# Transposing q of the first head pair of a batch by DMA instead of on TensorE, in a fused attention and feed-forward kernel

## The chip, the cores and the metric

The kernel runs on 1 core of one Trainium2 chip. The metric is the device time of one execution in microseconds (us), taken as the median of several runs. PE is TensorE, DVE is VectorE, ACT is ScalarE, POOL is GpSimd, and SP is the engine whose queue issues nearly all DMAs of this kernel.

## The reference

A thresholded attention over 8 batches and 8 heads of 576 rows and 64 columns feeds a two-layer block on 4608 rows of 512 columns. Cut to what matters:

```python
scores = (q @ k.transpose(0, 1, 3, 2)) / sqrt(64)        # per batch and head, 576 x 576
thresh = scores.max(-1, keepdims=True) - tau              # tau = 0.02
scores = where(scores >= thresh, scores, -1e9)
attn   = softmax(scores)
x      = (attn @ v), heads side by side                   # 4608 x 512
h      = x @ w_in                                         # 4608 x 2048
out    = (h - tanh(h)) @ w_out                            # 4608 x 512
```

## The kernel before

**Pairs, tiles and steps.** Two heads make a pair; there are 32 pairs p, four to a batch, so that pairs with `p % 4 == 0` are the first of a batch. A pair has nine tiles of 128 query rows: four of each head, and one that holds the last 64 rows of both (the shared tile). Tile i belongs to pair i // 9. A hand-written loop runs over steps s, and each step issues a piece of work for several tiles at once: `scores(s + 8)`, the kink of a tile three steps later, the exponential and the attention product of tiles further behind, and a share of the feed-forward work (`todo`). The order in which the loop issues is the order of every engine's queue; nothing is rescheduled afterwards.

**Preparing q and k.** `load` brings q, k and v of a pair from HBM through SP's queue. `split` (POOL, L189 to L193) scales the fp32 tile and writes it as two fp16 halves, high and low, into `qhl` or `khl`, so that 64 columns become 128. `turn` then transposes the nine 128 x 128 blocks. For k it does so on PE (L240, into the PSUM tile `ps_k`), DVE copies the result to `kT` (L263), and POOL makes a second copy with the two halves of the partitions exchanged, `kS` (L269, two instructions). For q there are two ways: like k through `ps_q` and a DVE copy to `qT`, or one DMA transpose straight from `qhl` to `qT` on SP's queue (L252). `q_by_dma(p)` chooses. The DMA writes the columns of the shared tile in another order, and `scores` reads them with a step of two (`qrem`).

**Scores and what follows.** A tile's scores are `kT` products followed by `kS` products into one PSUM tile `psS` (L331, L322 for the shared tile). DVE moves them to SBUF with the row maximum (L341) and derives the threshold `nb` (L353); ACT forms `z` (L368). From pair 6 on, two tiles' `z` are transposed by one DMA on SP's queue into `zT` (L375), and ACT takes the exponential into `pT` (L404), which PE multiplies with v (L425, L432, L443). The feed-forward block runs beside this: PE `psH` (L498), ACT `th` (L511), DVE `g` (L517), PE `psY` (L524). In each batch after the first it starts anew four steps after its first pair's step 0, so those four steps have no feed-forward work.

**When it is issued.** The table `PREP` and the lines behind it put `split` and `turn` into `plan`, at a distance d of steps ahead of step 9p - 8. For a pair p of 5 or more, `turn` of k stands at d = 6 for odd and d = 3 for even pairs. `turn` of q stands at d = 2, or at d = 7 if it goes by DMA, and both splits then stand two steps earlier:

```python
if d in (7, 8) and q_by_dma(p):
    d = d + 2
...
d = 7 if q_by_dma(p) else 3 - (p == 1 or p >= 5)
```

An engine's queue runs in order, so an instruction that waits holds up those behind it. Buffers: `hl`, `qk` (qT, kT, kS) and `ps_big` (psS, ps_q, ps_k) have two each.

Of the kernel before, what the change touches and what calls it, by code (L numbers as in the profile page):

```python
# [18 lines left out]
def kernel(  # L19
# [26 lines left out]
    HPAIR = H // 2  # L46
# [196 lines left out]

    def q_by_dma(p):

        return p >= 2 * HPAIR and p % 4 != 0

    def turn(p, t):
        hl = hls.pop((p, t))
        if t == "q" and q_by_dma(p):  # L250
            m = mats[p, t] = qk_pool.tile([P, W], FP16, name=f"{t}T", tag=t)
            nc.sync.dma_start_transpose(  # L252
                out=m.rearrange("p (c r) -> p c r", c=TPP),
                in_=hl.rearrange("p c a d -> p (c a d)"),
            )
            return
        ps = ps_big.tile([P, W], FP16, name=f"ps_{t}", tag="big")
        for c in range(TPP):
            turn_chunk(
                ps[:, c * P : (c + 1) * P], c, hl[:, c, :, :].rearrange("p a d -> p (a d)")  # L260
            )
        m = qk_pool.tile([P, W], FP16, name=f"{t}T", tag=t)
        nc.vector.tensor_copy(out=m, in_=ps)  # L263
        mats[p, t] = m
        if t == "k":
            sw = qk_pool.tile([P, W], FP16, name="kS", tag="ks")
            for lo, hi in ((0, D), (D, 0)):
                o, i = sw[lo : lo + D, :], m[hi : hi + D, :]
                nc.gpsimd.tensor_copy(out=o, in_=i)  # L269
            mats[p, "ks"] = sw  # L270
# [37 lines left out]
    def scores(i):  # L308
# [6 lines left out]
        if hh is None:  # L315
            qrem = REM
            if q_by_dma(p):
                qrem = (slice(512, 640, 2), slice(513, 640, 2))
            for n, kk in enumerate((kT, kS)):
                for dst, srcs in ((main, MAIN), (rem, REM)):  # L320
                    for hh in range(2):
                        nc.tensor.matmul(  # L322
                            out=ps[64 * hh : 64 * hh + 64, dst],
                            lhsT=qT[:, qrem[hh]], rhs=kk[:, srcs[hh]],
                            start=(n == 0), stop=(n == 1),
                        )
        else:
            lhs = qT[:, (5 * hh + t) * P : (5 * hh + t + 1) * P]
            for n, kk in enumerate((kT, kS)):
                for dst, src in ((main, MAIN[hh]), (rem, REM[hh])):  # L330
                    nc.tensor.matmul(  # L331
                        out=ps[:, dst], lhsT=lhs, rhs=kk[:, src],
                        start=(n == 0), stop=(n == 1),
                    )
# [324 lines left out]
    for p in range(1, NPAIR):  # L659
        first = TPP * p - AHEAD  # L660
        for d, f in PREP[3 if p == 1 else 0 :]:
            d -= p == 1 and d in (3, 5)
            if d in (7, 8) and q_by_dma(p):
                d = d + 2
            if p in (2, 4):
                d = {8: 9, 7: 8, 5: 6}.get(d, d)
            elif d == 5 and p >= 5:
                d = 6 if p % 2 else 3
            plan.setdefault(first - d, []).append(lambda p=p, f=f: f(p))
        d = 7 if q_by_dma(p) else 3 - (p == 1 or p >= 5)  # L670
        d = 4 if p in (2, 4) else d
        plan.setdefault(first - d, []).append(lambda p=p: turn(p, "q"))
# [30 lines left out]
    for s in range(-AHEAD, NTILE + LAG + 3):  # L703
        p, j = divmod(max(s, 0), TPP)
# [107 lines left out]
```

## Time and profile before

| | |
|---|---|
| median of 3 runs | 533.78 us (533.04, 533.78, 533.81) |
| the profiled execution's own time | 533.81 us, span 532.0 us |
| mean granted TensorE clock | 0.996 |
| busy share of the span | PE 96%, ACT 82%, DVE 79%, POOL 55% |
| DMA transposes `zT<-z` | 117, median 3.5 us from issue to landing |
| DMA transposes `qT<-qhl` | 18, median 3.3 us from issue to landing |
| q transposes on PE (`ps_q`, nine blocks each) | 126 matmuls, 14 pairs |

How to read it: the busy share of PE is an average over the whole span. Rows of the timeline give the start, the length, the engine, the line, the operation and the tile, and in brackets the idle time just before it with what ended it. A row that merges several instructions ends with their count. A matmul's length in such a row holds its latency; from the start of one group to the start of the next is what it takes of PE.

### The profile page before, as it was taken

To read this page: it belongs to the slowest core of one execution; us is meant where nothing else is said; L and a number is where in the kernel's file an instruction comes from. 1 tells how busy PE (TensorE), PEld (TensorE's weight loads), DVE (VectorE), ACT (ScalarE), POOL (GpSimd) and SP (SyncE) were. 2 spreads that over 40 slices of the span, in tenths; PEclk is the share of its full clock that TensorE was granted. 3 is DMA by queue.
4 is the path that set the end of the run, shared out by engine and by line. 5 is a ranking of instruction groups with operands and counts; after the bars stand their busy time and mean duration, and the time that the engine had idled before them with its cause. 6 is when DMAs were issued, how large, how long until landed. Compare 5 with 4: busy or idle time off the path is not lost.

```text
span 532.0 us, 12716 instructions
## 1 busy us (share of the span) xinstructions
PE 509.2 (96%) x4606; PEld 287.6 (54%) x4606; DVE 421.0 (79%) x1179; ACT 435.8 (82%) x617; POOL 290.1 (55%) x390
## 2 busy tenths in 40 slices
PE   8999899988999999999999999999999999999996
PEld 4666566544555555555555555555555555444444
DVE  5899879996888988898889988898889887554440
ACT  5999899988898989898898989898989899543330
POOL 8999989683746657475727574666657530000000
PEclk9999999998999999999999999999999999999999
DMA  7843659979897999789898899999979996400113
GB/s 212 252 133 114 217 186 184 167 160 197 170 209 140 190 184 217 173 179 202 186 197 186 191 188 199 171 185 199 214 160 185 195 149 110 105 33 28 39 41 80
DMA packets 208607, 86.79 MB, mean 163 GB/s; under 512 B 176160, under 2 KB 200992, under 8 KB 208544
## 3 DMA queue, kind: packets, MB, share of 16 engines
q1 hardware_dynamic: 207952, 85.56, 76.0%
q8 instruction: 36, 0.59, 0.5%
q10 hardware_dynamic: 592, 0.43, 0.3%
q14 instruction: 27, 0.22, 0.1%
HBM read 36.70 MB, written 9.44 MB: 87 GB/s over the span
## 4 chain that ended last, share of the span: by engine, by line
PE 35%; issue 20%; POOL 19%; ACT 9%; DMA 8%; DVE 6%; SPq 2%; POOLq 0%; ACTq 0%; DVEq 0%
PE psY L524 12%; PE psH L498 9%; PE psS L331 6%; POOL kS L269 5%; DMA vraw<-in_v_dram 4%; ACT z L368 3%; ACT pT L396 3%; PE psHt L498 3%; DMA kraw<-in_k_dram 3%; POOL khl L193 3%; POOL vb L221 2%; POOL qhl L193 2%; ACT th L511 1%; POOL qhl L192 1%; PE psO L432 1%
## 5 line engine op out<-in xcount | busy, mean ns | idle before, releaser
L341 DVE TENSOR_SCALAR_CACHE_REDUCE sc<-psS 128x576 f32<-128x576 f32 x288 | 214.2, 753 | 39.8 <-PE psS L331 25.9
L368 ACT ACTIVATE z<-sc,nb 128x576 bf16<-128x576 f32 x288 | 216.4, 772 | 22.2 <-DVE nb L353 20.3
L524 PE MATMUL psY<-w_out_sb,g 128*128 128x512 bf16 (+1 forms) x592 | 145.9, 373 | 0.8 <-DVE yo L537 0.8
L404 ACT ACTIVATE pT<-zT 128x1152 f16<-128x1152 bf16 x117 | 135.2, 1156 | 13.4 <-DMA zT<-z 13.2
L269 POOL COPY kS<-kT 64x1152 f16<-64x1152 f16 x62 | 70.9, 1144 | 125.9 <-DVE nb L353 124.4
L498 PE MATMUL psH<-xT,w_in_sb 128*128 128x512 bf16 x480 | 124.1, 381 | 2.6 <-DVE g L517 2.5
L331 PEld LDWEIGHTS <-qT 128*128 128x128 f16 x1024 | 74.8, 98 | 62.3 <-issue 8.4
L331 PE MATMUL psS<-kT,qT 128*128 128x512 f16 (+1 forms) x512 | 104.6, 286 | 3.2 <-DVE sc L341 1.2
L517 DVE SCALAR_TENSOR_TENSOR g<-th,psH 128x512 bf16<-128x512 f32 x128 | 87.6, 684 | 20.9 <-ACT th L511 20.4
L331 PE MATMUL psS<-kS,qT 128*128 128x512 f16 x496 | 101.6, 286 | 1.7 <-POOL kS L269 1.6
L511 ACT ACTIVATE th<-psH 128x512 f32<-128x512 f32 x128 | 74.8, 585 | 22.4 <-PE psH L498 21.8
L524 PEld LDWEIGHTS <-g 128*128 128x128 bf16 x592 | 51.0, 98 | 56.9 <-issue 2.4
L498 PEld LDWEIGHTS <-w_in_sb 128*128 128x128 bf16 x576 | 49.4, 98 | 57.9 <-issue 6.0
L432 PE MATMUL psO<-vb,pT 128*128 128x65 bf16 x1024 | 53.5, 194 | 0.0
L432 PEld LDWEIGHTS <-pT 128*128 128x128 f16 x1024 | 44.4, 98 | 9.7
L193 POOL TENSOR_TENSOR qhl<-qraw,qhl 128x576 f16<-128x576 f32 x31 | 39.7, 1281 | 2.6
L193 POOL TENSOR_TENSOR khl<-kraw,khl 128x576 f16<-128x576 f32 x31 | 39.7, 1281 | 2.6
L396 ACT ACTIVATE pT<-psZ 128x512 f16<-128x512 bf16 (+1 forms) x54 | 35.2, 655 | 3.9 <-PE psZ L387 3.5
L537 DVE COPY yo<-psY 128x512 f32<-128x512 f32 (+1 forms) x31 | 21.2, 682 | 14.1 <-PE psY L524 12.4
L425 PE MATMUL psO<-vb,pT 128*128 128x130 bf16 x128 | 28.3, 221 | 3.3 <-ACT pT L404 2.7
L458 DVE TENSOR_TENSOR osb<-psO,rc 128x256 bf16<-128x256 f32 x64 | 27.2, 424 | 2.2
L263 DVE COPY kT<-ps_k 128x1152 f16<-128x1152 f16 x31 | 23.3, 753 | 4.1 <-PE ps_k L240 4.1
(79 smaller groups left out, 508.8 us busy)
## 6 DMA issues: line engine op xcount, KB each, us to landing
vraw<-in_v_dram SPq DMA_DIRECT2D x32, 256.0 KB, 4.0
out_dram<-yo SPq DMA_DIRECT2D x32, 256.0 KB, 2.8
kraw<-in_k_dram SPq DMA_DIRECT2D x31, 256.0 KB, 3.2
qraw<-in_q_dram SPq DMA_DIRECT2D x31, 256.0 KB, 3.4
wt<-in_moe_w_in_dram SPq DMA_DIRECT2D x8, 512.0 KB, 4.6
wt<-in_moe_w_out_dram SPq DMA_DIRECT2D x8, 512.0 KB, 3.9
zT<-z SPq DMA_TRANSPOSE x117, 3.5
qraw<-in_q_dram SPq DMA_DIRECT2D x32, 32.0 KB, 3.3
```

The costliest lines, as they stand in the source:

```text
L193: nc.gpsimd.tensor_tensor(out=hl[:, :, 1, :], in0=x, in1=hl[:, :, 0, :], op=ALU.subtract)
L269: nc.gpsimd.tensor_copy(out=o, in_=i)
L331: nc.tensor.matmul(out=ps[:, dst], lhsT=lhs, rhs=kk[:, src], start=(n == 0), stop=(n == 1),)
L341: nc.vector.tensor_scalar(out=sc, in0=ps[:, lo : lo + S], scalar1=SC, scalar2=None, op0=ALU.mult, op1=ALU.max, accum_out=mx[:, c : c + 1],)
L368: nc.scalar.activation(out=z, in_=sc, func=ACT.Prelu, bias=nb, scale=1.0, alpha=STEEP)
L396: nc.scalar.activation(out=pt[:, off * P : (off + n) * P], in_=ps[:, 0 : n * P], func=ACT.Exp)
L404: nc.scalar.activation(out=pt[:, 0 : n * P], in_=zts.pop(i)[:, 0:n, :], func=ACT.Exp)
L432: nc.tensor.matmul(out=po[:, t - 1 + ab, :], lhsT=pt[:, blk * P : (blk + 1) * P], rhs=vb[:, hh, c, :], start=False, stop=(n == 7), skip_gr ...
L498: nc.tensor.matmul(out=ps, lhsT=w_in_sb[:, c, n * P : (n + 1) * P], rhs=xs[m][:, c, :] if m < B else xR[:, c, :, :], start=(c == 0), stop= ...
L511: nc.scalar.activation(out=th, in_=ps, func=ACT.Tanh)
L517: nc.vector.scalar_tensor_tensor(out=gs[m][:, n, :], in0=th, scalar=-1.0, in1=ps, op0=ALU.mult, op1=ALU.add,)
L524: nc.tensor.matmul(out=ps, lhsT=gs[m][:, n, ms * P : (ms + 1) * P], rhs=w_out_sb[:, n, cols], start=(n == 0), stop=(n == DF_C - 1),)
```

## The change

`q_by_dma` no longer excludes the first pair of a batch. From pair 8 on, all pairs take the DMA path for q. This concerns six pairs: 8, 12, 16, 20, 24 and 28. Their `turn` of q leaves PE and DVE, becomes one DMA transpose on SP's queue, and moves from d = 2 to d = 7; their two splits move from d = 8 and 7 to d = 10 and 9; and their shared tile reads `qT` with a step of two.

```diff
     def q_by_dma(p):
 
-        return p >= 2 * HPAIR and p % 4 != 0
+        return p >= 2 * HPAIR
```

## The prediction

> **What bounds the kernel now.** I read the page first, for the shares:
>
> ```profile
> PE 509.2 (96%) x4606; PEld 287.6 (54%) x4606; DVE 421.0 (79%) x1179; ACT 435.8 (82%) x617; POOL 290.1 (55%) x390
> ```
>
> PE is nearly always busy, so PE work that goes should shorten the run, unless PE soon meets a wait. So I went to PE's timeline around the q of pair 12, one of the six:
>
> ```profile
> 159.55 0.67 PE L240 MATMUL ps_k<-ident_f,khl 128*128 128x128 f16 x9
> ...
> 161.41 0.67 PE L240 MATMUL ps_q<-ident_f,qhl 128*128 128x128 f16 x9
> 161.91 0.41 PE L331 MATMUL psS<-kT,qT 128*128 128x512 f16 x2
> ...
> 163.58 0.41 PE L331 MATMUL psS<-kT,qT 128*128 128x512 f16 x2
> 163.82 0.41 PE L331 MATMUL psS<-kS,qT 128*128 128x512 f16 x2
> ```
>
> No row has a bracket: PE never waits here. The nine q blocks take 161.91 - 161.41 = 0.50 us. But they stand between `turn` of k (159.55) and the first product that needs `kS` (163.82, tile 108). POOL's and DVE's timelines show when `kS` is there:
>
> ```profile
> 160.32 0.76 DVE L263 COPY kT<-ps_k 128x1152 f16<-128x1152 f16 x1 [0.38 <-PE ps_k L240]
> 161.15 2.33 POOL L269 COPY kS<-kT 64x1152 f16<-64x1152 f16 x2 [9.19 <-DVE nb L353]
> ```
>
> It ends at 163.48, only 0.34 us ahead of its use. Two pairs on, where q already goes by DMA, PE does wait for it:
>
> ```profile
> 190.91 0.41 PE L331 MATMUL psS<-kS,qT 128*128 128x512 f16 x2 [0.33 <-POOL kS L269]
> ```
>
> Such a wait stands in every batch from there (190.91, 248.64, 306.26, 363.47, 420.67), and the copy ends 0.05 us before the product starts. What `kS` of pair 14 came from I followed back through DVE and ACT:
>
> ```profile
> 187.11 0.69 DVE L517 SCALAR_TENSOR_TENSOR g<-th,psH 128x512 bf16<-128x512 f32 x1 [0.21 <-ACT th L511]
> 187.71 0.75 DVE L263 COPY kT<-ps_k 128x1152 f16<-128x1152 f16 x1
> ```
>
> ```profile
> 181.22 1.17 ACT L404 ACTIVATE pT<-zT 128x1152 f16<-128x1152 bf16 x1 [0.15 <-DMA zT<-z]
> ```
>
> DVE copies `kT` late because it waits for tanh; ACT runs without a gap from 181.22, where it waited for a DMA transpose. So in each batch PE is met again by a chain through SP, ACT, DVE and POOL, and the question is how much of the 0.50 us lies on a path that goes round PE's q blocks.
>
> **What goes.** Six times nine blocks on PE, 0.50 us each (pairs 12, 16, 20, 24, 28 alike; pair 8 has 0.44 us of waiting before them as well), and six DVE copies of 0.76 us. DVE gains nothing by itself: it waits for PE again 3.5 us later (0.59 us at 165.62).
>
> **Cap by `kS`.** The start of first `kS` use minus the end of the copy is 0.34 us in each of pairs 12, 16, 20, 24 and 28. As PE starts 0.05 us after the copy where it waits, it can come forward by 0.34 - 0.05 = 0.29 us; the other 0.21 us become a wait at L331. The chain from `turn` of k to `kS` starts before the q blocks and does not shorten. That bounds the gain at 5 x 0.29 = 1.45 us.
>
> **What of the 0.29 us reaches the next wait.** DVE waits for PE at 165.62, ACT for DVE at 172.02 (0.29 us), so both follow PE. From there to `kT` of pair 14 ACT is back to back, and its exponentials must find their `zT` landed. The SP side does not follow: `qT` of pair 13 is issued at 169.08, when POOL has ended its split at 169.05, and POOL has worked without a gap from `kS` of pair 12, ahead of the q blocks. The fourth tile of each first pair is the tightest; its exponential starts after the landing by 0.10 us in pairs 12 and 20 (ACT waits 0.15 and 0.14 us), 0.24 in 16, 1.01 in 24, 0.58 in 28. A waiting exponential starts 0.08 to 0.10 us after the landing. So ACT can follow by 0 (12), 0.14 (16), 0 (20), 0.29 (24) and 0.29 (28): 0.72 us in all.
>
> **Pair 8: nothing.** PE stands still for 2.52 us soon after:
>
> ```profile
> 121.21 0.23 PE L425 MATMUL psO<-vb,pT 128*128 128x130 bf16 x1 [2.52 <-ACT pT L404]
> ```
>
> That exponential waited for a `zT` issued at 114.52, 3.0 us after its `z`, because SP was at `qT` and loads behind POOL's split of pair 9; this hangs on `turn` of k of pair 8, ahead of its q. A gain at 101.65, or a delay under 2.5 us, ends in this wait. The one exchange on POOL, the split of k of pair 8 before one weight cast, leaves the end of the split of q at 94.4; in the other pairs POOL's order stays as it is.
>
> **What comes: one DMA transpose on SP, six times.** It stands behind a `zT` and a store and ahead of the loads of the next pair, at about 152.7 for pair 12. It waits for POOL's split (ended 150.8) and the last reader of its buffer (scores at 147.1): both past, and POOL isn't paced by steps, so d = 10 and 9 change nothing there. Issuing takes SP 1.26 to 1.67 us (median 1.32). Behind it in SP's queue: k loads (used some 9 us later), `zT` of tile 99, loads of q and v, `zT` of tile 101. SP drains by waiting:
>
> ```profile
> SPq L375 <- ACT z L368: 5.0, 3, 3.1
> ```
>
> That is SP's waits from 160 to 172, 5.0 us against 1.32 (the least among the five is 2.2 us, before 341). Until then two `zT` come 1.3 us later. Their landings precede the exponentials by 2.7 us or more, but 1.40 us for tile 209, and PE uses the result another 2.7 us after the exponential. The transfer is 1152 packets of 256 bytes, 1.6 us of all 16 engines:
>
> ```profile
> 147.00:162.00 15.00, 14.68 (x136) 8.16 (x133) 12.12 (x34) 13.19 (x19) 5.62 (x8) 1.00 1.01 198
> ...
> 177.00:192.00 15.00, 14.44 (x139) 7.98 (x136) 13.06 (x39) 14.85 (x21) 8.31 (x12) 1.00 1.13 201
> ```
>
> The DMA share (last but one) would go from 1.01 to some 1.11, and at 1.13 a `zT` took up to 5.1 us instead of 3.2. Together up to 1.3 + 1.9 = 3.2 us, under 1.40 + 2.7. Cost between 0 and 0.5 us in each of five pairs; I take 0, as the slack is nearer. `qT` itself lands some 6 us before its first use. The step of two costs nothing: the shared tile's products start alike (last of eight 0.47 to 0.49 us after the first) in either kind of pair.
>
> The Trainium skill ("VectorE: DVE Perf Modes", sections The three transpose paths and Rules for kernel authors) speaks against the change: TensorE where PSUM will do, 390 ns for a 128 x 128 block against 1309 by DMA. For nine blocks that would be an estimated 3.5 against 11.8 us; the trace has 0.50 on PE and 3.3 to landing, so both are dearer there than here.
>
> **Sum.** 533.81 (the profiled execution: span 532.0 and 1.8 around it, 0.03 above the median) - 0.72 = 533.1 us.
>
> **Rivals.**
> *A, only `kS` limits.* If landings come 0.3 us earlier, ACT follows everywhere: 1.45 us, 532.4. For it: the slack in two pairs is a matter of 0.2 us. Against: ACT waits there now.
> *B, PE alone.* If `kS` came earlier too, 5 x 0.50 = 2.5: 531.3. Against: the wait in each pair with `p % 4 == 2`.
> *C, slower: SP does not drain.* If the 1.32 us are still there when the first pair's `zT` are issued (from 171 on), ACT, `g`, `kT` and `kS` come later one for one, less the slack: with 0.10, 0.24, 0.10, 1.01 and 0.58 that is 1.22 + 1.08 + 1.22 + 0.31 + 0.74 = 4.6 us, 538.4. It decides as soon as the backlog at tile 107 (167.5) is over 0.1 us. Against: the 5.0 us of waiting; for: SP is 3 to 5 us behind in the second pair of each batch, and DMA is near full. This is also the form that the skill's rule would take, the dearer path showing.
> *D, none of it arrives:* all five chains go round the q blocks, 533.8.
>
> **How the numbers follow.** Forecast 0.45, A 0.22, B 0.07, C or a part of it 0.16, D 0.10. About 0.2% (1.07 us) is what a measurement can tell from no change. Faster than 532.7: A, B and the lower edge of the forecast, 0.33. Slower than 534.8: C, 0.16. Within: 0.51. The likeliest case alone reaches from 532.4 to 533.8; the range goes on to half of B below and to parts of C above, 531.7 to 534.8, and leaves out 0.2.
>
> **What would show it.** Right: L240 `ps_q` gone after pair 7; a new wait of PE for `kS` of about 0.2 us at the first tile of pairs 12 to 28; the wait at pairs 14 to 30 kept, longer by what the batch didn't keep; the 2.5 us wait at 121 kept; `zT` of tiles 99 and 101 issued about 1.3 us later, tile 107 at once. Wrong: no wait for `kS` in pair 12 (B), or SP late at tile 107 and longer waits of ACT for `zT` (C).

## The result, and the profile after

The changed kernel is slower: 537.94 us (median of 4 runs, 537.25 to 538.42) against 533.41 us (median of 4 runs of the kernel before beside it, 532.16 to 533.81). The ratio is 1.0088, with a 95% interval of 1.0067 to 1.0109: 4.5 us where the forecast was a gain of 0.7 us. The profiled execution of the changed kernel took 537.83 us, with a span of 536.0 us, 4.0 us longer than before. Of all executions reported below, one of the kernel e1_pe_kept took 647.44 us at a granted TensorE clock of 0.754; it counts in no median or ratio here, and another execution was traced in its place.

The page after, its row of the engines and two of its DMA queues:

```profile
PE 508.3 (95%) x4552; PEld 284.8 (53%) x4552; DVE 417.5 (78%) x1173; ACT 435.6 (81%) x617; POOL 290.1 (54%) x390
...
q1 hardware_dynamic: 215056, 87.33, 77.9%
q8 instruction: 35, 0.57, 0.4%
```

PE, DVE and ACT all do a little less than before, in a longer span: time was lost in waits. The 54 matmuls and 54 weight loads of six pairs are gone. Queue q8 had 36 packets before and has 35 now; it comes up again below. Its row before:

```profile
q8 instruction: 36, 0.59, 0.5%
```

PE's timeline around pair 12, in answer to the five lines of before:

```profile
158.97 0.66 PE L240 MATMUL ps_k<-ident_f,khl 128*128 128x128 f16 x9
...
162.49 0.41 PE L331 MATMUL psS<-kT,qT 128*128 128x512 f16 x2
162.95 0.41 PE L331 MATMUL psS<-kS,qT 128*128 128x512 f16 x2
```

From `turn` of k to the first `kS` product it was 163.82 - 159.55 = 4.27 us and is 162.95 - 158.97 = 3.98 us: 0.29 us shorter, to the figure of the prediction. The `kS` product now starts 0.46 us after the `kT` product instead of 0.24: the other 0.2 us is the new wait for `kS`. The same 0.29 us went in pairs 16, 20, 24 and 28. A further 0.58 us was gained around pairs 7 to 9. So the lead at this point is 0.87 us, and the step that shortens PE did what was forecast.

The loss stands behind it, in ACT's waits for `zT`. ACT's waits between 165 and 450 us (in total, times, longest), before:

```profile
ACT pT L404 <- DMA zT<-z: 10.3, 9, 1.9
```

and after:

```profile
ACT pT L404 <- DMA zT<-z: 16.7, 10, 3.5
```

The first of these waits is the one that the prediction had named, the exponential at 181.22 us, then with a wait of 0.15 us. ACT's timeline after:

```profile
181.32 1.17 ACT L404 ACTIVATE pT<-zT 128x1152 f16<-128x1152 bf16 x1 [1.12 <-DMA zT<-z]
```

ACT came 0.87 us earlier, but the exponential could not start before its DMA transpose had landed, 0.1 us later than before. So the lead of this batch is gone, and the prediction's outcome for pair 12 (0 of 0.29 us) came true. Its reason did not: it had the transpose issued and landing as before. The issue came 0.37 us earlier (175.65 against 176.02), and the landing took 0.47 us longer (5.56 against 5.09).

What the prediction did not have is the second kind of wait: the third tile of the second pair of each batch (tiles 119, 155, 191, 227, 263). From pair 17 on its exponential starts later in each batch. For tile 155, before and after:

```profile
252.09 1.17 ACT L404 ACTIVATE pT<-zT 128x1152 f16<-128x1152 bf16 x1 [1.48 <-DMA zT<-z]
```

```profile
253.19 1.17 ACT L404 ACTIVATE pT<-zT 128x1152 f16<-128x1152 bf16 x1 [2.81 <-DMA zT<-z]
```

DVE and PE of the changed kernel show how this reaches PE:

```profile
256.21 0.69 DVE L517 SCALAR_TENSOR_TENSOR g<-th,psH 128x512 bf16<-128x512 f32 x1 [1.44 <-ACT th L511]
```

```profile
256.95 1.02 PE L498 MATMUL psH<-xT,w_in_sb 128*128 128x512 bf16 x4 [0.81 <-DVE g L517]
```

The late exponential makes the `th` behind it on ACT late, `g` on DVE waits 1.44 us for `th`, and PE waits 0.81 us for `g`, since the buffer of `psH` is not free. PE's waits for `g` between 165 and 450 us, before and after:

```profile
PE psH L498 <- DVE g L517: 1.8, 6, 0.3
```

```profile
PE psH L498 <- DVE g L517: 4.8, 9, 0.8
```

The five cases together, from the two traces:

| tile | 119 | 155 | 191 | 227 | 263 |
|---|---|---|---|---|---|
| issue to landing of `zT`, before (us) | 4.94 | 4.79 | 4.53 | 4.03 | 3.87 |
| after | 5.75 | 5.54 | 5.40 | 5.40 | 5.93 |
| ACT's wait ahead of the exponential, before | 1.85 | 1.48 | 1.29 | 0.81 | 1.95 |
| after | 1.82 | 2.81 | 2.50 | 3.16 | 3.47 |
| start of that exponential, after minus before | +0.07 | +1.10 | +1.77 | +3.80 | +4.51 |

The last row is the loss: it grows by 0.7 to 2.0 us in each batch from pair 17 on, which takes the 0.29 us gained there with it. The start of pair 31 (DVE's pass L341 over its first scores) is 4.51 us later, too. So the question for the experiments is why these transposes take 5.6 us on average instead of 4.43.

**A suspect.** Queue q8 carries packets of 16,384 bytes. Their number follows the length of PE's program: before, 4606 matmuls and 4606 weight loads are 9212 instructions, and 9212 / 256 = 36.0 (36 packets); after, 9104 / 256 = 35.6 (35). So a packet of q8 is taken to be a read of the next 256 PE instructions, 64 bytes each; there is one about every 14 us, and each takes 0.9 to 1.9 us. Transposes that overlap such a read between the end of their issue and their landing land later: before 4.53 us (25 of 135, median) against 3.41 us without one; after 4.75 us (44 of 141) against 3.51. The reads of before drift through the batch, since a batch has 1034 PE instructions, 4 x 256 + 10. After it has 18 fewer, 1016, 4 x 256 - 8 (with PE's six semaphore instructions of a batch, 1040 and 1022). From 165 to 450 us the reads of after stay at nearly one place in each batch: one began 3.2 to 3.9 us after the issue of each of the five `zT` above, before it had landed.

### The profile page after: what moved, and what is told of

The parts are those of the page before. It is cut to its first block, busy times and chain, and to the rows that moved or that the text cites. A ratio compares the mean times of both kernels' runs of the same rounds, so it can differ in the third digit from the quotient of the medians.

```text
span 536.0 us, 12603 instructions
## 1 busy us (share of the span) xinstructions
PE 508.3 (95%) x4552; PEld 284.8 (53%) x4552; DVE 417.5 (78%) x1173; ACT 435.6 (81%) x617; POOL 290.1 (54%) x390
## 4 chain that ended last, share of the span: by engine, by line
PE 34%; ACT 22%; issue 18%; POOL 10%; DMA 10%; DVE 5%; SPq 1%; POOLq 0%; ACTq 0%; DVEq 0%
PE psY L524 11%; ACT z L368 10%; PE psH L498 8%; PE psS L331 6%; ACT pT L404 6%; DMA zT<-z 5%; ACT th L511 3%; POOL kS L269 3%; ACT pT L396 3%; PE psHt L498 3%; DMA vraw<-in_v_dram 2%; DMA kraw<-in_k_dram 2%; PE psO L432 1%; DVE sc L341 1%; PE psZ L387 1%
## 5 line engine op out<-in xcount | busy, mean ns | idle before, releaser
L341 DVE TENSOR_SCALAR_CACHE_REDUCE sc<-psS 128x576 f32<-128x576 f32 x288 | 214.3, 754 | 41.8 <-PE psS L331 29.1
```

Of the source, the lines that this page charges most:

```text
L341: nc.vector.tensor_scalar(out=sc, in0=ps[:, lo : lo + S], scalar1=SC, scalar2=None, op0=ALU.mult, op1=ALU.max, accum_out=mx[:, c : c + 1],)
```

## The experiments

Two theories. The *code theory*: the loss comes from PE's code reads, which now meet the transposes that ACT, and through it PE, waits for; the number of PE instructions decides, not what they do. The *load theory*: the six added transposes crowd SP and the DMA engines. In e3 to e7 matmuls on 64 columns of zeros stand ahead of the attention product of tile 73, in the 2.5 us that PE waited before 121.21 us. Each is two PE instructions (weight load and matmul), so later reads fall at an earlier place in the work.

**e1_pe_kept**: the changed kernel, with the nine q blocks still transposed on PE into a `ps_q` that nobody reads. The PE program has its old length, the DMA transposes stay, and DVE's six copies stay away. The blocks stand at d = 7, some steps earlier than before.

```diff
         if t == "q" and q_by_dma(p):
             ...
+            if p % 4 == 0:
+                ps = ps_big.tile([P, W], FP16, name=f"ps_{t}", tag="big")
+                for c in range(TPP):
+                    turn_chunk(
+                        ps[:, c * P : (c + 1) * P], c,
+                        hl[:, c, :, :].rearrange("p a d -> p (a d)"),
+                    )
             return
```

> The changed kernel, but PE also still transposes q of pairs 8, 12, ..., 28 into ps_q, and nobody reads it: the DMA transposes are added, PE's program keeps its length and its 0.50 us per pair. Load theory (the six added transposes crowd SP's queue and the DMA engines): as slow as the changed kernel, 537.5 to 539 us. Code theory (PE's code is read in 16 KB blocks on the DMA engines, and the 18 PE instructions fewer per batch put these reads onto the zT transfer that PE waits for): the reads fall as in the kernel before, 533 to 534.5 us, and the zT of the third tile of the second pair of a batch land 3.9 to 4.9 us after their issue instead of 5.4 to 5.9.

Measured: 532.49 us (11 executions), ratio 0.9987 (0.9973 to 1.0). With six DMA transposes more and no PE work less, the loss is gone, so the load theory falls. The trace is from a further execution:

> A second look at the changed kernel with PE's q transposes kept beside the DMA transposes, for its trace: code theory, zT of the third tile of the second pairs land 3.9 to 4.9 us after issue as in the kernel before, 532 to 534 us.

Measured: 531.65 us in one execution. The five `zT` land in 5.19, 4.39, 4.94, 4.30 and 3.47 us (mean 4.46, before 4.43), and from 165 to 450 us 16 transposes overlap a read (before 18, after 33).

**e2_no_dma**: the kernel before, without the nine q blocks and the DVE copy of these six pairs, and without the DMA transposes: such a pair uses the `qT` of the pair before it. The PE program has the length of the changed kernel.

```diff
+        if t == "q" and p >= 2 * HPAIR and p % 4 == 0:
+            mats[p, t] = mats[p - 1, t]
+            return
```

> The kernel before, without the PE transposes and DVE copies of q of pairs 8, 12, ..., 28 and without a DMA in their place: those pairs use q of the pair before them. PE's program is as short as in the changed kernel, no transfer is added. Load theory: faster than before, by 0.7 to 1.5 us, 532 to 532.7 us. Code theory: slow like the changed kernel, 536 to 538 us, with the same zT landing 5.4 us or more after issue.

Measured: 536.57 us, ratio 1.0073 (1.0052 to 1.0095). Work is only taken away, nothing is added, and the kernel gets slower nearly as much as by the whole change. The row of the engines from its page, ACT's waits for `zT` from 165 to 450 us, and tile 155 on ACT:

```profile
PE 507.9 (95%) x4552; PEld 285.1 (53%) x4552; DVE 417.0 (78%) x1173; ACT 435.0 (81%) x617; POOL 290.0 (54%) x390
```

```profile
ACT pT L407 <- DMA zT<-z: 15.0, 9, 2.9
```

```profile
253.43 1.16 ACT L407 ACTIVATE pT<-zT 128x1152 f16<-128x1152 bf16 x1 [2.80 <-DMA zT<-z]
```

The counts on PE are those of the changed kernel, the wait of 2.80 us is that of the changed kernel (2.81), and there is no added transpose. The five `zT` land in 4.86, 5.54, 5.26, 4.49 and 5.45 us: later than before on average (5.12 against 4.43), but only two of them at 5.4 us or more, as the code theory had expected of all. The two experiments are a cross: the loss goes with the length of the PE program, not with the transposes. In both, however, PE's time goes along with that length, 0.50 us a pair. The next experiments change the length and leave the work of the pairs as it is.

**e3_before_97** and **e4_after_54**: the program is moved with the real work as it was, by 194 instructions in the kernel before and by 108 in the changed kernel. The zeros cost next to nothing: 97 of them take 3.0 us, and the product behind them starts at 121.28 us instead of 121.21. The edit, with 97 or 54:

```diff
+            if i == 73:
+                for _ in range(54):
+                    nc.tensor.matmul(
+                        out=ops[p, hh][:, 0, 0:64], lhsT=zero[:, 0:P], rhs=zero[:, 0:64],
+                        start=True, stop=True, skip_group_check=True,
+                    )
```

> The kernel before, with 97 matmuls of 64 columns on zeros (194 PE instructions, an estimated 2.7 us at 28 ns) put where PE waits 2.52 us for pT of tile 73; q as before. Load theory: nothing, 533.3 to 533.9 us. Code theory: the code reads come some 3.4 us later against the work of the later batches, onto the same zT as in the changed kernel: 535 to 538 us.

Measured: 535.72 us, ratio 1.0047 (1.0032 to 1.0062): slower, as the code theory said. Four of the five `zT` land later than before (4.02, 5.61, 5.18, 5.33 and 4.44 us).

> The changed kernel, with 54 such matmuls (108 PE instructions, an estimated 1.5 us) at the same place, where it waits 1.01 us and 1.06 us a little later. Load theory: nothing, 537.5 to 538.5 us. Code theory: the code reads come some 6 us earlier against the work and leave those zT: 532 to 534.5 us.

Measured: 529.37 us, ratio 0.9929 (0.9916 to 0.9942), faster than the code theory expected, and faster than both kernels: some 8.5 us less than the changed kernel (by the two ratios), which does the same work without the zeros. In it the product behind the zeros starts 0.77 us later than in the changed kernel (120.66 us), and the next of its kind 0.46 us earlier (123.94). From its page, q8, and ACT's waits for `zT` from 165 to 450 us:

```profile
q8 instruction: 36, 0.59, 0.5%
```

```profile
ACT pT L404 <- DMA zT<-z: 7.2, 7, 1.6
```

The five `zT` land in 3.73, 3.92, 3.85, 3.64 and 3.55 us, although all six added transposes are there, and only 9 transposes overlap a read from 165 to 450 us (after: 33). So the added transposes by themselves do not make these five land late.

**e5_before_32** and **e7_after_27**: the same edit with 32 in the kernel before and with 27 in the changed kernel, half of e4's.

> The kernel before with 32 matmuls on zeros (64 PE instructions) in PE's wait for pT of tile 73; q as before. Code theory: the code reads come some 3.5 us earlier against the work of the later batches and leave the zT of the second pairs: faster than before, and slower than the changed kernel with 54 such matmuls (529.4) by what the change itself is worth, 5 x 0.29 = 1.45 us: 530.8 us, between 530.2 and 531.6. Load theory: as before, 533.1.

Measured: 532.05 us, ratio 0.9958 (0.9943 to 0.9974). Faster, as expected, but by less than the code theory's range. Start of pair 31: 434.89 us against 432.80 in e4. Of these 2.09 us, 1.45 are the q blocks (five times 0.29); most of the rest is one stretch, from the start of pair 14 to that of pair 15 (15.61 us against 14.81). Ahead of it a read met the `zT` of tile 117 (5.48 us to its landing): ACT waited 0.81 us for it, against 0.01 us in e4 (5.05 us), and the exponential of tile 119 came 0.98 us later.

> The changed kernel with half the padding, 27 matmuls (54 PE instructions). Code theory: code reads some 3 us earlier than in the changed kernel, so that they fall into the first half of the same zT, as in the kernel before: between the 537.9 of no padding and the 529.4 of 54, 531 to 535 us. Load theory or an effect of the padding's place: 529.4 or 537.9, one of the two.

Measured: 532.28 us, ratio 0.9971 (0.9955 to 0.9988), between the changed kernel and e4, as expected; the five `zT` take 4.55, 4.65, 4.51, 5.36 and 5.05 us. An effect of the place of the zeros alone would have given the time of one of the two.

**e6_after_54_k**: e4, with `turn` of k of pairs 12, 16, 20, 24 and 28 one step earlier, to take away the new wait for `kS`.

```diff
+                if p >= 12 and p % 4 == 0:
+                    d = 4
```

> The changed kernel with 54 matmuls on zeros, and k of pairs 12, 16, 20, 24 and 28 transposed one step earlier on PE (d = 4 in place of 3). If the cap by kS is real (0.21 us of PE's 0.50 us per pair are spent waiting for kS), five waits of 0.4 us on the page's row of kS go and the run takes 529.4 - 5 x 0.21 = 528.3 us, or less where more of the wait goes. If kS did not hold PE, nothing: 529.4.

Measured: 529.56 us, ratio 0.9916 (0.9901 to 0.9931), which is e4 (0.9929), not the 528.3 us expected. PE's timeline at pair 12:

```profile
161.84 0.41 PE L331 MATMUL psS<-kT,qT 128*128 128x512 f16 x2
162.08 0.41 PE L331 MATMUL psS<-kS,qT 128*128 128x512 f16 x2
```

The wait is gone (0.24 us between the two), and each of the five stretches that end with the start of one of these pairs is 0.21 us shorter (15.28 to 15.07). But pair 31 starts at 432.80 us in both kernels. ACT's waits for `zT` are 10.1 us instead of 7.2, and two stretches are longer (from pair 14: 15.58 us instead of 14.81; from pair 26: 15.18 instead of 14.85): PE's lead is given back where ACT waits for a landing, as at 181.32 above. This is read from two traces, not tested further.

All together, the nine traces, sorted by time (the overlaps do not sort them strictly; it may also matter which transposes are met); overlaps counted from 165 to 450 us. The medians come from three sessions, in which the kernel before had 533.41, 533.09 (e1 to e4) and 533.98 us (e5 to e7). By the ratios the order is the same but for e4 and e6, which can't be told apart.

| kernel | median (us) | transposes that overlap a read | mean landing of the five `zT` (us) |
|---|---|---|---|
| e4 | 529.37 | 9 | 3.74 |
| e6 | 529.56 | 11 | 3.75 |
| e5 | 532.05 | 18 | 3.90 |
| e7 | 532.28 | 21 | 4.82 |
| e1 | 532.49 | 16 | 4.46 |
| before | 533.41 | 18 | 4.43 |
| e3 | 535.72 | 22 | 4.92 |
| e2 | 536.57 | 25 | 5.12 |
| after | 537.94 | 33 | 5.60 |

The place of a transpose in the batch could itself make it land late, with or without a read. So each `zT` is compared with the same `zT` in the other traces: from 165 to 450 us, 80 of 88 have a read in the 3.3 us behind their issue in some of the nine traces and not in others. In 77 of the 80 the landing takes longer on average with the read than without, by 0.73 us in the mean over the 80.

What stays open: the reads were moved, never taken away, so that a read lengthens a transpose rests on nine traces in which the overlap moves with the instruction count, not on a run without reads. A second queue of the kind instruction, q14, has 26 or 27 packets of 8,192 bytes in each page; no run moved these on purpose, and what they cost a transpose is not shown. Whether the added transposes cost anything by themselves can't be told: e2, without them, has 1.0073 and the changed kernel 1.0088, with overlapping intervals. And the gain of the change with the reads out of the way was not isolated: e4 and e5 (0.9929 and 0.9958) differ by about 1.5 us, the size of 5 x 0.29, but their reads lie at different places.

## Why the prediction was wrong, and where it was right

**Right: the cap by `kS`.** 0.29 us in each of five pairs, a new wait of 0.2 us at the first tile, the waits at pairs 14 to 30 kept (0.33 us at 191.00, as before). For pair 12 the lead was lost at the exponential at 181 us, as the step "What of the 0.29 us reaches the next wait" had it, but with some luck: SP did follow by 0.37 us, and the landing took 0.47 us longer.

**Right in the main, and without effect: SP.** `zT` of tiles 99 and 101 were issued 1.74 and 1.53 us later behind their `z` than before, against 1.3 forecast, and tile 107 at once (0.03 us after its `z`). Tile 103 was late as well, by 1.06 us, where the forecast had two late `zT` and no third. SP's waits from 160 to 172 us after:

```profile
SPq L375 <- ACT th L511: 3.2, 2, 2.4
SPq L375 <- ACT z L368: 1.5, 2, 1.0
```

SP still drains there, so **rival C** did not happen. Its 538.4 us is near the 537.9 measured by luck: its place was the backlog at tile 107, and there is none.

**The other rivals.** B is excluded: `kS` did not come earlier, PE waits for it. A and D, and the forecast's own 0.72 us beyond pair 12, can't be told apart, because the later landings cover what ACT would have followed by.

**Off by 0.58 us: "Pair 8: nothing".** The wait at 121.21 did not stay at 2.52 us; it became two on PE, of about 1 us each:

```profile
119.89 0.23 PE L425 MATMUL psO<-vb,pT 128*128 128x130 bf16 x1 [1.01 <-ACT pT L404]
...
124.40 0.23 PE L425 MATMUL psO<-vb,pT 128*128 128x130 bf16 x1 [1.06 <-ACT pT L404]
```

That is the 0.58 us gained by pair 12, where nothing was forecast.

**Wrong: "What goes".** This is the step that failed first. It priced six times nine blocks as PE time alone. They are also 108 PE instructions, and the length of PE's program sets where its reads of code fall. No term of the sum held that, and the q8 row of the page, which shows these reads, was passed over. e2 measures the omission: 1.0073, or 3.9 us more, for taking away the blocks and their copies and adding nothing.

**Wrong: "Cost between 0 and 0.5 us in each of five pairs; I take 0".** The bound was made for tiles 99, 101 and 209 and for the DMA share, which was to rise to 1.11 in the stretch from 147 to 162 us. The windows after:

```profile
147.00:162.00 15.00, 14.68 (x129) 7.84 (x127) 12.13 (x35) 13.20 (x20) 5.58 (x9) 1.00 1.02 199
...
177.00:192.00 15.00, 14.07 (x127) 7.46 (x124) 12.45 (x37) 13.88 (x20) 7.43 (x11) 1.00 1.06 194
```

The share is 1.02 in the first stretch (1.01 before, 1.11 forecast) and 1.06 in the second (1.13 before). The DMA engines were hardly fuller on average; single transposes met a read. And the tile that had no room left, the third of the second pair, whose exponential already waited 0.81 to 1.95 us for its `zT` in all five batches, was not priced at all: the prediction looked for slack that might be used up, at the fourth tile of the first pair, and not at the waits that existed and could only grow. It was put at 0, and these landings grew by 1.17 us on average (4.43 to 5.60 us). ACT's waits for `zT` grew by 6.4 us in all (10.3 to 16.7). Of these, 0.87 us and four times 0.29 us took back the leads; the 4.4 us that are left are about the 4.51 us by which pair 31 starts later.

## What to carry to other kernels

Instructions taken away or added on an engine also move its reads of code, and where a transfer is already waited for, that can be worth more than their time: here some 8.5 us between e4 and the changed kernel, which do the same work, against 3 us for all six sets of nine blocks. Before a small edit is judged, try it beside two or three numbers of idle instructions in a wait that costs nothing; if the time jumps with the number, it is the place that is measured, not the edit. And price first the waits that the profile already shows for a transfer, since a later landing reaches the end from there without any slack.

## What the runs showed of the hardware

Each read on q8 is one packet of 16,384 bytes, 35 to 37 of them here, which by the counts above is one for 256 PE instructions; it lies among the kernel's transfers. A DMA transpose of two `z` tiles that overlaps one takes 4.5 to 4.9 us (medians of the nine traces) against 3.4 to 3.5 us without, and the sixteen parts in which the landing is reported can be late together (tile 155 after: the first part at 5.28 us, the last at 5.54), though a read is a single packet. The Trainium skill ("Runtime: NRT & Kernel Launch", section Instruction fetch mechanics) says that an engine's instruction memory is refilled in 16 KiB blocks of 256 instructions over a DMA queue of its own, which the counts here agree with, and that crossing a block costs one queue bump, mostly hidden. For PE itself that may hold; no run here tests it. For the transposes beside the read it does not hold here: 1.1 to 1.5 us lie between the medians, and 529.4 against 537.9 us between e4 and the changed kernel.

A read every 256 instructions also means that a batch whose program is close to a multiple of 256 (1016 here, against 1034 before) meets its reads at nearly the same place again and again. The effect then repeats: in e4 no read met any of the five `zT`, in the changed kernel a read met all five.
